# Unread products of 512 columns on TensorE behind the attention stages of a fused attention and two-layer MoE kernel

## The chip, the cores and the metric

One core of a Trainium2 chip runs the whole program. The metric is the device time of one execution in microseconds, the median of several runs. Engines are named as the profile names them: PE (TensorE's products), PEld (its weight loads), DVE (VectorE), ACT (ScalarE), POOL (GpSimd) and SP (the engine that issues most DMAs).

## The reference

Three parts run one after the other, and the output of each feeds the next:

```python
# attention: B=4, H=8, S=768, D=40; the state is D x D for each of 32 (batch, head) units
for t in range(S):
    y[:, :, t] = einsum('bhd,bhde->bhe', rt, state)
    Sa = einsum('bhde,bhe->bhd', state, at)
    state = state * wt - einsum('bhd,bhe->bhde', Sa, bt) + einsum('bhd,bhe->bhde', vt, kt)
# dense: x is y as 3072 x 320; w_in 320 x 2048, w_out 2048 x 320
h = x @ w_in
x = maximum(0.01 * h, h) @ w_out
# experts: each token goes to the one expert of eight with the largest logit
expert_idx = argmax(x @ w_gate); gate_w = softmax(x @ w_gate) at that expert
out[mask] = gate_w[mask] * (maximum(xe @ w1[e], 0) @ w2[e])
```

## The kernel before

The 768 time steps are cut into 24 chunks of 32. For a chunk `c` the work comes in two kinds. The **preparation** (`prep`, `prep_b`, `prep_c`) doesn't depend on the chunk before: scans of the decays on DVE, the scaled keys, and then two groups of small products on PE (L265, each group 16 matmuls for half of the units), which DVE and ACT take out of PSUM (L269, L271) and SP writes to memory. The **attention stages** carry the state from one chunk to the next. In the order of their use they are `s1` (L399), `s2` (L414; for chunks under 8 it is three products in a row, with an ACT copy and a DVE sum between them), `s3x` (L457), `s3` in two halves (L439), `s4` in two halves (L469), `s5` in two halves (L486) and `s6` in two halves (L504). Each is one bank of small matmuls with at most 104 rows and 80 columns of the array, followed by a copy on ACT or DVE that the next stage needs. A triangular inverse for every group of chunks (L301 to L366, on POOL, for the first group on DVE) gives the matrix `TT` that `s2` uses.

The **dense phase** is the first MoE layer, done in 12 groups of 256 tokens and 16 blocks of the hidden dimension: `layer1` is eight matmuls of 128x128 weights by 256 columns (L722), and `layer2` six of 320 columns (L738). Its weights come in as 64-bit words and are turned into pairs of float32 on DVE and ACT (L569 to L658); this conversion runs from the start of the program beside the attention. The second MoE layer (L1146, L1162) ends the program.

The order on every engine is written out by hand. `overlap` plays a string of words, `START`, and then one string for every later chunk: `s1.0` is stage `s1` of chunk 0, `0G` a piece of the preparation of chunk 0, `p` the next piece of the preparation of the chunks from 4 on, `+` a piece of the weight conversion, and `H` half a block of the dense phase. `done` counts the words `H` played so far, so it is 0 until the first one, which stands behind `s5a.2` in `START`. In the profiled execution the first product of `layer1` starts at 133.42 us. Instructions of one engine run in the order in which they were written.

A helper `keep_warm` stands in the code before, with two products, called by a word `F` that no string contains: it puts no instruction into the program. PSUM has the pool `psX` with the tags `psX0` and `psX1`, one bank each, which `layer2` sums into; nothing uses it before the first `layer2`.

Of the kernel before, what the change touches and what calls it, by code (L numbers as in the profile page):

```python
# [12 lines left out]
F32 = mybir.dt.float32  # L13
# [1233 lines left out]
def build(tc, i, out, dbg=None):  # L1247
    nc = tc.nc
    with ExitStack() as top:
# [10 lines left out]
        with ExitStack() as left, ExitStack() as ctx, ExitStack() as right:  # L1260
            psH = ctx.enter_context(tc.tile_pool(name="psH", bufs=2, space=PSUM, side="right"))
            m1 = Moe1(tc, ctx, i, k, xT, x2d, tbl, psH)
            with ExitStack() as ctx2:
                psA = ctx2.enter_context(tc.tile_pool(name="psA", bufs=4, space=PSUM))
                at = Attn(tc, ctx2, i, k, xT, bad, psA)
                own, m1.bank = m1.bank, at.bank
                half, routing = overlap(tc, at, m1, plan)
                m1.bank = own
            m2 = Moe2(tc, left, right, i, k, x2d, tbl, out, plan)

            bs = cst.tile([128, 1], F32, name="bs")
            nc.vector.tensor_reduce(out=bs, in_=bad, axis=AX.X, op=ALU.add)

            def check():
                ps = m1.bank()
                nc.tensor.matmul(ps[0:1, 0:1], bs, k.one, start=True, stop=True)
                nc.vector.tensor_single_scalar(badi[0:1], ps[0:1, 0:1], 0.0, op=ALU.is_gt)
                nc.vector.tensor_single_scalar(plan.bad, ps[0:1, 0:1], 0.0, op=ALU.is_gt)

            tail(m2, half, check)  # L1280
            m1.inner.close()
            m2.banks(m1.bank)
            m2.more()
            m2.go(routing, plan.make(m1))
# [8 lines left out]
                m2.other(lo, hi)  # L1293


def keep_warm(at, m1):

    ps = at.bank()
    for _ in range(2):
        at.nc.tensor.matmul(ps.rearrange("q (a b) -> q a b", a=4), m1.ones, m1.ones[:, None, :].to_broadcast([128, 4, 128]), start=True, stop=True)  # L1300


def overlap(tc, at, m1, plan):

    nc = tc.nc
    ws = m1.weights(at.bad[:, NC:])
    units = m1.units()
    routing, inv, hurry = [], [], []
    done = owed = 0

    def more(n):
        for _ in range(n):
            next(ws, None)


    at.scratch(m1.lend())
    for c in range(2):
        at.load1(c)
        at.load1b(c)
    at.load1b(2)  # L1320
    P = {}

    def prep():

        for c in range(4, NC):
            for n, f in enumerate(at.prep(c)):
                if n == 14 and c % 4 == 0:
                    while c // 4 - 1 not in at.read:
                        (inv if c > 4 else hurry).pop(0)()
                f()  # L1330
                if n == 3 and c + 1 < NC:
                    at.load1(c + 1)
                if n == 14:
                    if c < NC - 1:
                        at.load1b(c + 1)
                yield
            if c % 4 == 3:
                inv.extend(at.halves(1, 0, 32, nc.gpsimd) if c == 7 else at.inverse(c // 4, nc.gpsimd))

    todo = prep()  # L1340

    def half():

        nonlocal done, owed
        if done % 2 == 0:
            more(owed)
            owed = 0
            while m1.within or not m1.want(done // 2):
                next(ws, None)
            m1.flush()  # L1350
        if done == 0:
            m1.split_x()
        if done == 2 * NF:
            for _ in ws:
                pass
            m1.rows(9)
            m1.late()
        g = done // (2 * NF)
        new = next(units, None)
        if new is None:  # L1360
            return False
        done += 1
        routing.extend(new)
        if routing:
            routing.pop(0)()
            if not routing and g in EARLY:
                plan.early(m1, EARLY[g])
        if done % (2 * NF) == LOAD and g + 1 < NC // 2:
            m1.load_x(m1.xT[g + 1].rearrange("f c n -> f (c n)"))
        if done % (2 * NF) == SPLIT and g + 1 < NC // 2:  # L1370
            m1.split_x()
        return NF * NC + 3 - done

    def play(order, here=0):


        nonlocal owed
        turns, k = order.count("w"), 0
        for word in order:
            what, _, c = word.partition(".")  # L1380
            c = here + int(c or 0)
            if what[0].isdigit():
                n = int(what[0])
                if n not in P:
                    P[n] = at.prep(n)
                P[n]["abcdefGgHhIiJjz".index(what[1])]()
            elif what == "H":
                half()
            elif what == "+":
                if done % 2:  # L1390
                    owed += 1
                else:
                    more(1)
            elif what == "p":
                next(todo, None)
            elif what == "u":
                if hurry:
                    hurry.pop(0)()
            elif what == "v":
                if inv and not hurry:  # L1400
                    inv.pop(0)()
            elif what == "w":
                for _ in range(-(-len(inv) // (turns * (4 - here % 4) - k))):
                    inv.pop(0)()
                k += 1
            elif what == "L":
                at.load1(c)
            elif what == "K":
                at.load1b(c)
            elif what in "VP":  # L1410
                at.mul = nc.vector if what == "V" else nc.gpsimd
            elif what == "A":
                hurry.extend(at.halves("a", 0, 16, nc.vector))
            elif what == "B":
                hurry.extend(at.halves("b", 16, 32, nc.gpsimd))
            elif what == "C":
                m1.clear()
            elif what == "F":
                keep_warm(at, m1)
            elif what in "Ee":  # L1420
                more(what == "E")
            elif what in "gd":
                m1.low = nc.gpsimd if what == "g" else nc.vector
            elif what == "x":
                m1.load_x(m1.xT[0].rearrange("f c n -> f (c n)"))
            elif what in ("l2", "l3"):
                if c < NC:
                    (at.load2 if what == "l2" else at.load3)(c)
            elif what[2:] in ("a", "b"):
                if what[1] != "3" or c < NC - 1:  # L1430
                    getattr(at, what[:2])(c, "ab".index(what[2]))
            else:
                if what == "s2":
                    while (c // 4 if c > 3 else "ab"[c // 2]) not in at.TT:
                        (inv if c > 3 else hurry).pop(0)()
                getattr(at, what)(c)

    play(START.split())
    for c in range(5, NC):
        play((STEP if c < NC - 5 else LATE if c < NC - 1 else END).split(), c)  # L1440
    return half, routing
# [35 lines left out]
```

## Time and profile before

| What | Value |
|---|---|
| median of 3 runs | 1090.9 us (1087.32 to 1091.97) |
| the profiled execution, its own time | 1100.18 us |
| its span, first to last instruction | 1098.4 us |
| PE busy in the span | 929.3 us (85%) |
| DVE busy in the span | 807.6 us (74%) |
| mean granted clock of TensorE | 0.951 |
| first product of the dense phase | 133.42 us |

The profiled execution took 9.3 us more than the median of the runs, and 1.8 us of it lie outside its span. Busy time is the time in which an engine has at least one instruction under way. "Idle before" names what the engine waited for last. The granted clock is a column of its own in some views: 1.00 stands for TensorE's upper level of 2.4 GHz and 0.50 for its lower level of 1.2 GHz.

### The profile page before, as it was taken

The page shows a single profiled execution, that of the slowest core. Times are in us where ns is not written, and L with a number is a line of the kernel's source. Part 1 is how long each engine was busy: PE and PEld are TensorE (multiplying, and loading weights), DVE is VectorE, ACT ScalarE, POOL GpSimd, SP SyncE. Part 2 cuts the span into 40 slices and gives each one's busy share as a digit, 9 for nine tenths or more (in the row PEclk, how much of TensorE's full clock was granted, in tenths as well). Part 3 has the DMA queues.
Part 4 walks back from the last instruction along what each step waited for, and adds up shares of the span by engine and source line. Part 5 has one row for each costly group of instructions (what it writes and reads, how often), then busy time and mean ns, then how long its engine had stood idle before and what let it go on. Part 6 is the DMA issues. An engine that isn't in the chain of part 4 may idle for free.

```text
span 1098.4 us, 40672 instructions
## 1 busy us (share of the span) xinstructions
PE 929.3 (85%) x16854; PEld 871.4 (79%) x16854; DVE 807.6 (74%) x1900; ACT 531.3 (48%) x1316; POOL 512.3 (47%) x690
## 2 busy tenths in 40 slices
PE   2265778878799888889889998999999799999995
PEld 1255667777788878878779887998899699999995
DVE  8988788866778786868787666567656777877771
ACT  3545554663334444444435443444446466666661
POOL 5124145215873399447964585333556432332221
PEclk9999986888889999999999998999999899999998
DMA  7878876856546555575656442332425537354440
GB/s 250 228 213 228 227 208 178 232 149 172 151 114 173 140 162 159 141 169 138 158 151 144 124 78 73 91 82 55 151 90 140 204 129 246 100 169 146 140 126 16
DMA packets 143991, 166.04 MB, mean 151 GB/s; under 512 B 67931, under 2 KB 105451, under 8 KB 143671
## 3 DMA queue, kind: packets, MB, share of 16 engines
q1 hardware_dynamic: 133687, 144.20, 47.9%
q10 hardware_dynamic: 5760, 10.49, 3.3%
q0 software_dynamic: 4352, 8.69, 2.5%
q8 instruction: 134, 2.20, 0.9%
q14 instruction: 58, 0.48, 0.2%
HBM read 127.62 MB, written 42.27 MB: 155 GB/s over the span
## 4 chain that ended last, share of the span: by engine, by line
PE 42%; DVE 24%; DMA 9%; issue 9%; POOL 8%; ACT 6%; SPq 1%; POOLq 0%; DVEq 0%; ACTq 0%
PE psH L722 9%; PE psX L738 8%; PE epy L1162 8%; PE psH L1146 6%; DVE junk L762 3%; PE eph L1146 3%; DVE g L727 2%; POOL itmp L309 2%; POOL Tinv L315 2%; DMA L<-dKBr 2%; PE psA L414 2%; POOL gl L729 2%; DVE lam L226 1%; PE psA L486 1%; DVE Rr L472 1%
## 5 line engine op out<-in xcount | busy, mean ns | idle before, releaser
L729 POOL TENSOR_TENSOR gl<-g,gh 128x256 fp32r<-128x256 f32 x192 | 156.9, 820 | 221.4 <-ACT gh L728 186.7
L727 DVE TENSOR_TENSOR g<-psH,g 128x256 f32<-128x256 f32 x192 | 81.2, 423 | 108.2 <-ACT g L726 97.3
L728 ACT CAST gh<-g 128x256 fp32r<-128x256 f32 x192 | 78.2, 407 | 163.6 <-DVE g L727 156.7
L738 PE MATMUL psX<-woh,gh 128*128 128x320 f32 x384 | 134.0, 349 | 1.3 <-ACT woh L649 1.1
L738 PE MATMUL psX<-woh,gl 128*128 128x320 f32 x384 | 124.9, 325 | 6.9 <-POOL gl L729 6.6
L726 ACT ACTIVATE g<-psH 128x256 f32<-128x256 f32 x192 | 73.8, 384 | 109.0 <-PE psH L722 89.6
L738 PE MATMUL psX<-wol,gh 128*128 128x320 f32 x384 | 123.3, 321 | 0.0
L762 DVE SCALAR_TENSOR_TENSOR junk<-X,raws 128x320 bf16<-128x320 f32 x160 | 93.3, 583 | 4.6 <-ACT X L759 2.7
L722 PE MATMUL psH<-xh,wih 128*128 128x256 f32 x384 | 87.4, 311 | 4.9 <-DVE g L727 4.0
L309 POOL TENSOR_TENSOR itmp<-Tinv 128x30 f32<-128x30 f32 (+14 forms) x120 | 72.8, 607 | 33.9 <-DVE Tinv L301 26.7
L738 PEld LDWEIGHTS psX<-woh,gl 128*128 128x128 f32 x384 | 76.3, 199 | 10.2 <-POOL gl L729 9.7
L722 PE MATMUL psH<-xl,wih 128*128 128x256 f32 x384 | 81.3, 295 | 0.0
L722 PE MATMUL psH<-xh,wil 128*128 128x256 f32 x384 | 80.9, 294 | 0.0
L738 PEld LDWEIGHTS psX<-woh,gh 128*128 128x128 f32 x384 | 76.3, 199 | 5.4 <-ACT woh L649 1.3
L265 PE MATMUL psA<-AtI,KB 40*64 40x72 f32 x1408 | 43.9, 264 | 42.3 <-DVE KB L243 18.9
L1174 POOL DMA_INDIRECT out<-ey,sid x32 | 33.3, 1041 | 97.2 <-ACT ey L1173 91.7
L315 POOL TENSOR_TENSOR Tinv<-Tinv,itmp 128x30 f32<-128x30 f32 (+14 forms) x120 | 73.7, 614 | 7.8
L738 PEld LDWEIGHTS psX<-wol,gh 128*128 128x128 f32 x384 | 76.8, 200 | 0.3 <-DVE wol L650 0.3
L265 PEld LDWEIGHTS psA<-AtI,KB 40*64 40x64 f32 x1408 | 35.5, 163 | 49.7 <-POOL woh L242 18.3
L722 PEld LDWEIGHTS psH<-xh,wih 128*128 128x128 f32 x384 | 66.3, 201 | 10.1 <-DVE g L727 6.5
L1150 DVE SCALAR_TENSOR_TENSOR ehl<-psH,ehh 128x256 fp32r<-128x256 f32 x86 | 36.2, 421 | 41.5 <-ACT ehh L1149 38.6
L722 PEld LDWEIGHTS psH<-xl,wih 128*128 128x128 f32 x384 | 63.6, 203 | 0.3 <-DVE xl L707 0.3
(292 smaller groups left out, 2775.5 us busy)
## 6 DMA issues: line engine op xcount, KB each, us to landing
raw<-hwe SPq DMA_DIRECT2D x48, 512.0 KB
raw<-hwe SPq DMA_DIRECT2D x32, 640.0 KB
in<-h SPq DMA_DIRECT2D x23, 521.0 KB
KB<-h SPq DMA_DIRECT2D x22, 512.0 KB
L<-dKBr SPq DMA_DIRECT2D x24, 320.0 KB
dKBr<-KBr SPq DMA_DIRECT2D x22, 320.0 KB
lamY<-dl SPq DMA_DIRECT2D x24, 264.0 KB
dl<-lam SPq DMA_DIRECT2D x22, 264.0 KB
```

The costliest lines, as they stand in the source:

```text
L265: nc.tensor.matmul(box[i][64 * j:64 * j + 64, k, :], z["KB"][o, p, :], z["AtI"][o, p, :], start=True, stop=True)
L309: eng.tensor_tensor(out=box["v"], in0=T[:, k + 1:32, k:k + 1].to_broadcast([128, n, k]), in1=T[:, k:k + 1, 0:k].to_broadcast([128, n, k]), ...
L315: eng.tensor_tensor(out=T[:, k + 1:32, 0:k], in0=T[:, k + 1:32, 0:k], in1=box["v"], op=ALU.add)
L722: nc.tensor.matmul(ps[:, 0:256], w, x, start=(n == 0), stop=(n == 7))
L726: nc.scalar.activation(out=g, in_=ps[:, 0:256], func=AF.Copy, scale=0.01)
L727: nc.vector.tensor_tensor(out=g, in0=ps[:, 0:256], in1=g, op=ALU.max)
L728: nc.scalar.copy(out=gh, in_=g)
L729: return gh, gl, lambda: nc.gpsimd.tensor_tensor(out=gl, in0=g, in1=gh, op=ALU.subtract)
L738: nc.tensor.matmul(s.x2[t][:, 0:DM], x[:, o], w[:, f, :], start=(f == 0 and n == 0), stop=(f == NF - 1 and n == 2))
L762: nc.vector.scalar_tensor_tensor(out=s.junk, in0=X[:, t, 0:DM], scalar=1.0, in1=s.wg[:, e], op0=ALU.mult, op1=ALU.mult, accum_out=lg[:, t, ...
L1146: nc.tensor.matmul(ps, w, x, start=(n == 0), stop=(n == 7))
L1162: nc.tensor.matmul(s.y[t][:, 0:DM], x[:, o], w, start=(f == 0 and n == 0), stop=(f == 7 and n == 2))
```

## The change

`keep_warm` now takes the bank `psX0` and makes three products into it. The stationary operand is a 128x128 tile of ones in bfloat16, the moving operand the same tile read four times, 512 columns. Nobody reads the result. The helper is called behind both groups of products of every preparation, and behind every attention stage that `play` plays, for as long as no `H` has been played. The word `F` is gone.

```diff
-def keep_warm(at, m1):
-    ps = at.bank()
-    for _ in range(2):
-        at.nc.tensor.matmul(ps.rearrange("q (a b) -> q a b", a=4), m1.ones, m1.ones[:, None, :].to_broadcast([128, 4, 128]), start=True, stop=True)
+def keep_warm(m1):
+    ps = m1.psX.tile([128, 512], F32, name="psX0", tag="psX0")
+    for _ in range(3):
+        m1.nc.tensor.matmul(ps.rearrange("q (a b) -> q a b", a=4), m1.ones, m1.ones[:, None, :].to_broadcast([128, 4, 128]), start=True, stop=True)
...
                 f()
+                if n in (6, 10) and not done:
+                    keep_warm(m1)
...
                 P[n]["abcdefGgHhIiJjz".index(what[1])]()
+                if what[1] in "GI" and not done:
+                    keep_warm(m1)
...
-            elif what == "F":
-                keep_warm(at, m1)
...
                     getattr(at, what[:2])(c, "ab".index(what[2]))
+                    if not done:
+                        keep_warm(m1)
...
                 getattr(at, what)(c)
+                if not done:
+                    keep_warm(m1)
```

On PE this makes 45 groups of three, 135 products and 135 weight loads. The order of all other engines is the same as before, and so is PE's own beside the added instructions. On PE, from stage `s2` of chunk 0 to its first half of `s3`, there stand before:

```order
L399 MATMUL psA<-Vx_178,At 32x40 x32
L414 MATMUL psA<-RH,TT 32x40 x32
L414 MATMUL psA<-Xq,NT 32x40 x32
L414 MATMUL psA<-RH,TT 32x40 x32
L457 MATMUL psA<-ident,Xq 128x128 x4
L439 MATMUL psA<-Vx_178,L_180 40x40 x16
```

The same place as a difference, from the last product of `s2` (RH, TT) to `s3x` (ident, Xq), where `ones` is the tile of ones and `psX_825` the unread bank:

```order
 L414 MATMUL psA<-RH,TT 32x40 x32
 L414 MATMUL psA<-Xq,NT 32x40 x32
 L414 MATMUL psA<-RH,TT 32x40 x32
+L1300 LDWEIGHTS ones
+L1300 MATMUL psX_825<-ones 128x512
+L1300 LDWEIGHTS ones
+L1300 MATMUL psX_825<-ones 128x512
+L1300 LDWEIGHTS ones
+L1300 MATMUL psX_825<-ones 128x512
 L457 MATMUL psA<-ident,Xq 128x128 x4
```

Nothing stands between the three products of `s2`; the group comes behind the last. The last of the 45 groups stands on PE between the first half of `s5` of chunk 2 (L486) and the first product of the dense phase (L722):

```order
 L486 MATMUL psA<-Rr,L_180 40x32 x16
+L1300 LDWEIGHTS ones
+L1300 MATMUL psX_2214<-ones 128x512
+L1300 LDWEIGHTS ones
+L1300 MATMUL psX_2214<-ones 128x512
+L1300 LDWEIGHTS ones
+L1300 MATMUL psX_2214<-ones 128x512
 L722 MATMUL psH<-xh,wih 128x256 x2
```

From there on PE's order is that of before.

## Rows read from the trace of the kernel before

**Rows 1.** Page: busy tenths of PE and DVE in 40 slices of the span.
```profile
PE   2265778878799888889889998999999799999995
...
DVE  8988788866778786868787666567656777877771
```
**Rows 2.** Stretches: window, length, busy PE, PEld, DVE, ACT, POOL; clock, DMA share, GB/s.
```profile
18.30:53.50 35.20, 11.96 (x320) 10.08 (x320) 31.25 (x84) 16.20 (x48) 5.89 (x6) 1.00 0.80 212
61.70:133.40 71.70, 47.59 (x1484) 41.15 (x1484) 61.35 (x134) 39.43 (x108) 19.18 (x36) 1.00 0.84 227
133.40:202.20 68.80, 55.36 (x1245) 49.22 (x1246) 55.79 (x118) 37.33 (x103) 26.83 (x45) 0.75 0.75 202
```
**Rows 3.** Stretches between changes of the granted clock, same columns.
```profile
0.00:147.50 147.50, 74.97 (x2364) 64.90 (x2364) 124.83 (x277) 70.34 (x190) 44.17 (x83) 1.00 0.82 228
...
151.00:157.80 6.80, 6.08 (x79) 6.01 (x80) 6.43 (x17) 5.93 (x19) 4.49 (x11) 0.50 0.64 150
...
164.60:168.00 3.40, 3.40 (x32) 3.07 (x33) 3.40 (x5) 1.51 (x6) 2.21 (x3) 0.50 0.41 132
...
178.30:202.20 23.90, 20.22 (x435) 18.13 (x436) 18.03 (x42) 13.46 (x38) 4.95 (x8) 0.50 0.76 208
```
**Rows 4.** PE timeline 53 to 164: start, us, engine, line, out<-in [idle before <-releaser].
```profile
53.54 1.29 PE L414 MATMUL psA<-RH,TT 32*32 32x40 f32 x64 [4.19 <-DVE TT L366]
...
61.73 1.11 PE L457 MATMUL psA<-ident,Xq 128*128 128x128 f32 x4 [2.48 <-ACT Xq L427]
...
66.41 1.29 PE L439 MATMUL psA<-Vx,L 64*40 64x40 f32 x32 [0.33 <-DVE Vx L445]
67.47 1.28 PE L486 MATMUL psA<-Rr,L 64*40 64x32 f32 x32
...
77.71 1.29 PE L414 MATMUL psA<-RH,TT 32*32 32x40 f32 x64 [0.89 <-ACT RH L401]
...
81.52 1.29 PE L414 MATMUL psA<-RH,TT 32*32 32x40 f32 x64 [0.61 <-DVE RH L422]
...
163.10 0.46 PE L469 MATMUL psA<-Rr,Vt 40*32 40x32 f32 x32 [2.25 <-ACT Vt L459]
```
**Rows 5.** PE timeline: layer-2 products at the lower, then upper level; stages at the upper.
```profile
191.41 0.47 PE L738 MATMUL psX<-wol,gh 128*128 128x320 f32 x1
191.68 0.47 PE L738 MATMUL psX<-woh,gl 128*128 128x320 f32 x1
...
309.85 0.31 PE L738 MATMUL psX<-woh,gl 128*128 128x320 f32 x1
310.00 0.30 PE L738 MATMUL psX<-woh,gh 128*128 128x320 f32 x1
...
312.03 0.79 PE L439 MATMUL psA<-Vx,L 64*40 64x40 f32 x32
```
**Rows 6.** Whom PE waited for, 61.7 to 133.4: total us, times, longest.
```profile
PE psA L469 <- DMA Vt<-hvt: 4.3, 1, 4.3
PE psA L457 <- ACT Xq L427: 4.3, 2, 2.5
PE psA L399 <- issue: 2.6, 2, 1.4
...
PE psA L265 <- issue: 1.6, 1, 1.6
...
PE psA L265 <- POOL Tinv L358: 1.4, 1, 1.4
```
**Rows 7.** Whom DVE waited for, 61.7 to 133.4, same columns.
```profile
DVE Vx L426 <- PE psA L414: 2.8, 2, 1.4
```
**Rows 8.** Whom PE waited for, 133 to 235, same columns.
```profile
PE psA L414 <- ACT Xq L419: 5.7, 3, 4.6
PE psA L414 <- DVE RH L422: 4.9, 3, 2.4
...
PE psA L486 <- DMA L<-Z: 0.3, 1, 0.3
```

## The prediction

> **What bounds the kernel now.** I read the page's slices first [rows 1]: in the first five slices (some 137 us) DVE is the fuller engine, PE is half full, and from about the seventh slice on PE is at eight tenths or more. The 45 groups of unread products all lie in the first 133.4 us, so that stretch has to be weighed by itself. Between 61.7 and 133.4 us DVE is busy 61.35 of 71.7 us (86%) and PE 47.59 (66%), and from 133.4 to 202.2 us PE is busy 55.36 of 68.8 [rows 2]. DVE being full doesn't make PE free there: the longest of DVE's own waits in this stretch is for PE's `s2` [rows 7], and `s2` waits in turn for copies on ACT and DVE [rows 4]. The two hand work to each other in a fixed order, and a stage that PE makes late makes DVE late.
>
> The granted clock has to be read with care. The column says 1.00 from 0 to 147.5 us [rows 3]. The durations say otherwise: 64 products of `s2` take 1.29 us at 53.5 us and again at 77.7 [rows 4], and half an `s3` takes 1.29 us at 66.4 [rows 4] against 0.79 at 312 [rows 5], where the column shows the upper level too. So all of the stretch in question runs at the lower level, 1.2 GHz, and the first recorded change comes behind it. The Trainium skill (TensorE: Matmul & The Clock Gate, Part 1: The HAM clock gate) says that the lower level is the state an unworked TensorE starts in, and that its clock records are not fully to be trusted; the durations here agree with that and not with the column. By the column alone the change could only cost: the groups at the upper level's price, with no stage to shorten.
>
> **The change part by part.** Price of a group. No row shows a 512-column product of bfloat16. The nearest rows are `layer2`'s, 128x128 weights by 320 columns: at the lower level they start 0.27 us apart (191.41, 191.68), at the upper 0.15 (309.85, 310.00) [rows 5]. In proportion to the columns that is 0.43 and 0.24 us for 512, so a group of three costs 1.28 us at the lower level and 0.70 at the upper. The weight loads are inside those spacings, so I add nothing for them; a fresh load ahead of each group could add some 0.1 us. I take 1.28 and 0.70.
>
> What hides it. A group is free as far as PE would have waited anyway. 10 groups come before 61.7 us and 35 between there and 133.4. Of these 35 places 16 have a wait of PE behind the stage in the trace before; each can hide at most one group. The longest three are for the `Vt` transfer (4.3 us), for `Xq` (two of 4.3 together; the group behind `s2` of chunk 0 is one of the two) and for the inverse (1.4) [rows 6]. Summed place by place, with each wait capped at a group's length, 12.4 us are hidden at the lower level (1.28 each for the three long ones of 4.29, 1.79 and 1.40, and 0.2 to 1.14 for the other 13) and 9.5 at the upper. The waits inside `s2`, one of them 0.61 us in chunk 1 [rows 4], hide nothing, since no group stands there. The other 19 places have no wait: PE goes straight on, as from `s3` at 66.41 to `s5` at 67.47 [rows 4], and there the whole group pushes the next stage.
>
> At the lower level throughout: 35 x 1.28 = 44.8, less 12.4, is 32.4 us that the stretch grows by. What is left of the three long waits over a group (3.0 + 0.5 + 0.1) and two waits inside stages (1.6 and 1.4 us) [rows 6] can take up lateness from earlier, if what they wait for isn't late itself: 32.4 - 3.6 - 3.0, about 26 us at the least. I take 29.
>
> At the upper level throughout: 35 x 0.70 = 24.5, less 9.5, is 15.0 us more. The stages become shorter: 0.79 for 1.29 is 0.61 [rows 5], so 47.59 us of PE work [rows 2] would shrink by 18.6 us. If all of this counted, the stretch would end 3.6 us earlier; if half of it does, because DVE is full beside it, 5.7 us later. I take +1.
>
> The first 10 groups. In 18.3 to 53.5 us PE is busy only 11.96 of 35.2 [rows 2], and the wait of 4.19 us ahead of the first `s2` [rows 4] takes up most lateness of PE; but that wait ends with the inverse, which begins with what the first four groups of products give. Two of the early groups stand where PE goes straight on. Bounds 0 and 3 us; I take 1.5. The group behind the first `s2` is covered by the 2.48 us ahead of `s3x` [rows 4].
>
> Which level it will be. In the trace before, PE working without a break on attention stages alone never left the lower level in 133 us. It rose at 157.8, 168.0 and 202.2, each time at the end of a stretch that is full of 128x128 products, after 6.8, 3.4 and 23.9 us at the lower level [rows 3]; it fell at 164.6 [rows 3], behind a wait of PE of 2.25 us [rows 4]. A group of 1.28 us behind stages of 1.08 to 1.29 us makes half of PE's time such products where it goes straight on, so I expect rises there. But every `s2` is 5 us without a group (77.71 to 82.81) with two waits in it [rows 4], and the transfer of `Vt` leaves 3 us idle even behind a group. These three breaks (4.3 + two of about 5.5 us), each with a climb of some 5 us behind it, estimated between the 3.4 and 6.8 us of [rows 3], make 30 of 71.7 us at the lower level: 0.4.
>
> The rule of the same page (section: Why this matters for your kernels) is to leave TensorE no idle gaps between bursts, which by itself would count any busy stretch and put all of this at the upper level. The rows don't bear it out for attention stages alone, and the sum by that rule is the second rival's.
>
> After the first `H` nothing is added. PE's waits from 133 to 235 us are for ACT and DVE in the order written out, the `Xq` copies (5.7 us) and the sums of `s2` (4.9) [rows 8], both of which are late by as much; for a DMA there is 0.3 us [rows 8]. So lateness at 133.4 us is carried to the end nearly whole, and I take it as whole. That the dense phase begins at the upper level can give 0 to 2 us back, taken as 0, since PE's clock goes its own way there from `s2` to `s2`.
>
> Sum: 1.5 + 0.4 x 29 + 0.6 x 1 = 13.7 us. The profiled execution would go from 1100.18 to some 1114 us; the median of the runs is 9.3 us lower, and the same 13.7 us on it give **1104 us**, +1.2%.
>
> **The rivals.** First, the groups don't raise the clock, so the change doesn't do what it says: 1.5 + 26 to 32 us, 1118 to 1125, near 1121. For it: PE without a break stayed at the lower level all through the stretch. Against it: half of the time would be 128x128 products. Second, the upper level holds in nearly all of the stretch, and DVE paces it: 1.5 - 3.6 to 1.5 + 5.7, 1089 to 1098; as far as it lies within 5.5 us of the median it is no change. Third, the other side, faster: the upper level holds and PE's stages pace the stretch, above all `s2`, whose three products have no group between them and each lose 0.5 us. Then the 18.6 us of shorter stages count whole, the groups' 15.0 are against them, `s2` of chunk 0 (three of 1.29 us before 61.7) gives 1.5 more, and the dense phase's first 14 us, in which PE works nearly without a break, run at the upper level, which gives up to 5: down to -10 us, 1081 to 1085. It decides from about the point where less than an eighth of the stretch is at the lower level (0.125 x 29 against 0.875 x -3.6, no net loss).
>
> **How the numbers follow.** The forecast (clock goes up and down, 1097 to 1114) 0.47; the first rival 0.18; the second 0.18; the third 0.17. Half a per cent, 5.5 us, is about what a measurement of this kernel can tell from no change. Faster by more than that: the third, 0.17. Within it: most of the second and a little of the forecast's lower end, 0.20. Slower: 0.63. The range leaves out the lower half of the third rival and the upper third of the first: 1084 to 1122. The likeliest case alone is 1097 to 1114.
>
> **What the profile after would show.** The first `layer1` product at about 147 us in place of 133.4 (after allowance for the run; 160 by the first rival, 130 by the third). Unread products that start 0.43 us apart in some stretches and 0.24 in others. `s2`'s three products at 1.29 us each in most chunks, since they are what falls. DVE's waits for PE between 61.7 us and the first `H` up by about 10 us. From there to the end the same length as before, within 3 us. The forecast would be wrong if a group costs far from 1.28 and 0.70 us; if the clock stays up through `s2`; or if the dense phase takes back the lateness, which would show as a shorter stretch from the first `H` to the end.

## The result: 7.5 us slower

| | kernel before | changed kernel |
|---|---|---|
| median | 1089.54 us (1084.68 to 1095.65, 15 runs) | 1097.02 us (1091.11 to 1106.12, 15 runs) |
| profiled execution | 1100.18 us | 1098.11 us |
| its span | 1098.4 us | 1096.2 us |
| mean granted clock | 0.951 | 0.924 |
| first product of the dense phase | 133.42 us | 143.22 us |

The ratio is 1.007, with a 95% interval of 1.0045 to 1.0096: slower by more than a measurement's spread, and by about half of the forecast 13.7 us (1104 us). The two profiled executions can't be compared by their spans: that of before was 10 us over its median. So both kernels were profiled a second time, and places are compared in pairs. The two mean clocks can't be compared either: in that of before the first 147.5 us count as 1.00 [rows 3], although the durations are those of the lower level.

The page of the changed kernel, busy tenths in 40 slices, against [rows 1]:

```profile
PE   3478868878888998898989999999999899999995
...
DVE  8977678767769697877788677667657767777771
PEclk9776877688889999998999999999999899999998
```

PE is fuller in the first five slices, and DVE is emptier from the third on. The clock row now has digits under 9 from the second slice on, where the page of before had 9 in all of the first five: the first recorded change is now a rise near 28 us, and from there on the column follows the durations. The longer windows that answer to [rows 2] (window, length, busy PE, PEld, DVE, ACT, POOL with counts; clock, DMA share, GB/s):

```profile
18.30:53.50 35.20, 19.65 (x347) 10.36 (x347) 29.33 (x83) 16.17 (x48) 6.18 (x6) 0.79 0.75 201
...
61.70:133.40 71.70, 60.52 (x1396) 34.84 (x1400) 52.07 (x114) 34.23 (x93) 19.27 (x36) 0.76 0.77 205
```

PE goes from 47.59 to 60.52 us in the second window and DVE from 61.35 to 52.07. The timeline of PE in the changed kernel (start, us, engine, line, out<-in, [idle before <-releaser]) has the groups at both levels, the first rise (the preparation's products take 1.24 us at 20.89 and 0.73 at 28.65), `s2` of chunk 1, and the first dense product:

```profile
19.50 1.46 PE L1300 MATMUL psX<-ones 128*128 128x512 bf16 x3
20.89 1.24 PE L265 MATMUL psA<-woh 40*64 40x72 f32 x32
...
28.65 0.73 PE L265 MATMUL psA<-wol 40*64 40x72 f32 x32
...
67.34 0.82 PE L1300 MATMUL psX<-ones 128*128 128x512 bf16 x3
68.09 0.76 PE L469 MATMUL psA<-Rr,Vt 40*32 40x32 f32 x64
...
80.54 0.90 PE L414 MATMUL psA<-RH,TT 32*32 32x40 f32 x64 [0.58 <-ACT RH L401]
82.45 1.01 PE L414 MATMUL psA<-Xq,NT 32*32 32x40 f32 x64 [1.01 <-ACT Xq L419]
84.04 1.54 PE L414 MATMUL psA<-RH,TT 32*32 32x40 f32 x64 [0.58 <-DVE RH L422]
85.52 1.46 PE L1300 MATMUL psX<-ones 128*128 128x512 bf16 x3
...
143.22 0.50 PE L722 MATMUL psH<-xh,wih 128*128 128x256 f32 x2 [0.82 <-ACT xh L706]
```

A group takes 1.39 us of PE's time at the lower level (19.50 to 20.89) and 0.75 at the upper (67.34 to 68.09). The upper level, reached in the run of stages from 64 us on, is lost over `s2` of chunk 1: its third product and the group behind it are at lower-level lengths again.

**Where the time came from.** The stretch from 61.7 us to the dense phase falls into two parts, cut at the start of `s3x` (L457) of chunks 0 and 1 and at the first `layer1` product. The kernel before, from its two profiles, the first profile ahead:

```profile
61.73:91.04 29.31, 21.64 (x693) 18.98 (x693) 25.16 (x56) 15.96 (x45) 10.54 (x24) 1.00 0.78 207
91.04:133.42 42.38, 25.96 (x792) 22.17 (x792) 36.18 (x79) 23.47 (x64) 8.64 (x13) 1.00 0.88 241
```
```profile
61.20:89.87 28.67, 21.65 (x693) 18.98 (x693) 24.95 (x56) 15.87 (x45) 10.81 (x25) 1.00 0.76 203
89.87:133.70 43.83, 25.99 (x793) 22.36 (x793) 35.58 (x80) 23.27 (x64) 8.95 (x12) 1.00 0.85 232
```

The changed kernel, the same parts, from its two profiles:

```profile
62.44:98.04 35.60, 31.95 (x741) 18.40 (x741) 25.98 (x59) 17.50 (x49) 11.76 (x28) 0.76 0.76 204
98.04:143.22 45.18, 36.16 (x851) 20.77 (x849) 33.36 (x77) 22.11 (x59) 7.51 (x8) 0.81 0.77 206
```
```profile
62.32:97.97 35.65, 31.68 (x740) 18.16 (x741) 25.94 (x59) 17.49 (x49) 11.65 (x28) 0.76 0.70 194
97.97:139.15 41.18, 35.95 (x850) 20.55 (x849) 34.01 (x77) 22.24 (x59) 7.57 (x8) 0.79 0.81 226
```

And the groups alone (L1300) in the first of these two profiles, PE busy in the third column:

```profile
62.44:98.04 35.60, 16.77 (x48) 3.99 (x48) 0.76 0.76 204
98.04:143.22 45.18, 19.51 (x58) 4.64 (x57) 0.81 0.77 206
```

The first part grew from 29.0 us (mean of two) to 35.6: +6.6 us. There 16 groups put in 16.8 us, and the stages gave 6.5 back (21.65 less 31.95 - 16.77 = 15.2). The net of 10.3 us met a PE that had stood idle for only 7.3 us (29.0 - 21.65) and still stands idle for 3.65 and 3.97. So about half of the idle time was used, and the rest of the 10.3 us lengthens the part. The second part has 19 groups, and its mean length is the same as before, 43.2 against 43.1 us: 19.5 us of groups less 9.4 us of shorter stages is a net of 10.1, and PE had stood idle there for 16.4 and 17.8 us, of which 9.0 and 5.2 are left. The two lengths after, 45.18 and 41.18, lie 4 us apart, so the zero is known to within some 2 us only. The starts of `s3x` vary less: by the means of two profiles each, the changed kernel is 7.5 us late at `s3x` of chunk 1 (98.0 against 90.5; 0.9 of it from before chunk 0's) and 7.1 at chunk 2 (129.5 against 122.4). So nearly the whole loss is one cycle of one chunk.

DVE's waits for PE in the first part, the kernel before and then the changed one (who waits <- for whom: total us, times, longest):

```profile
DVE Ms L269 <- PE psA L265: 1.0, 1, 1.0
```
```profile
DVE Ms L269 <- PE psA L265: 4.3, 3, 1.6
DVE Rr L472 <- PE psA L469: 1.9, 1, 1.9
```

Before, its wait for the preparation's products was one of 1.0 us and for `s4` none: DVE now waits for PE. The lateness is then carried. `s3x` of chunk 10 in the first profiles of before and after:

```profile
393.13 0.66 PE L457 MATMUL psA<-ident,Xq 128*128 128x128 f32 x4
```
```profile
400.03 0.66 PE L457 MATMUL psA<-ident,Xq 128*128 128x128 f32 x4
```

In the second ones it starts at 392.32 and 399.63: +7.1 us by the means, of the same size as the 7.5 us at the end.

### The profile page after: what moved, and what is told of

Its sections match the earlier page's. It is cut to its first block, busy times and chain, and to the rows that moved or that the text cites. A ratio compares the mean times of both kernels' runs of the same rounds, so it can differ in the third digit from the quotient of the medians.

```text
span 1096.2 us, 40926 instructions
## 1 busy us (share of the span) xinstructions
PE 955.7 (87%) x16989; PEld 867.2 (79%) x16989; DVE 805.6 (73%) x1900; ACT 530.3 (48%) x1316; POOL 512.4 (47%) x690
## 4 chain that ended last, share of the span: by engine, by line
PE 47%; DVE 19%; DMA 10%; POOL 9%; issue 8%; ACT 5%; SPq 1%; ACTq 0%; POOLq 0%; DVEq 0%
PE psH L722 9%; PE psX L738 9%; PE epy L1162 8%; PE psH L1146 6%; POOL itmp L309 3%; PE eph L1146 3%; POOL Tinv L315 3%; DVE junk L762 2%; PE psA L414 2%; POOL gl L729 2%; DVE g L727 2%; PE psA L265 2%; PE psX L1300 2%; PE psA L486 1%; PE psA L439 1%
## 5 line engine op out<-in xcount | busy, mean ns | idle before, releaser
L722 PE MATMUL psH<-xh,wih 128*128 128x256 f32 x384 | 87.0, 310 | 4.8 <-DVE g L727 3.8
L722 PE MATMUL psH<-xl,wih 128*128 128x256 f32 x384 | 80.9, 294 | 0.4 <-DVE xl L707 0.4
L722 PE MATMUL psH<-xh,wil 128*128 128x256 f32 x384 | 80.6, 293 | 0.0
L722 PEld LDWEIGHTS psH<-xh,wih 128*128 128x128 f32 x384 | 66.2, 200 | 10.1 <-DVE g L727 6.1
L265 PE MATMUL psA<-AtI,KB 40*64 40x72 f32 x1408 | 39.0, 252 | 33.9 <-DVE KB L243 18.8
L265 PEld LDWEIGHTS psA<-AtI,KB 40*64 40x64 f32 x1408 | 31.3, 152 | 46.3 <-POOL woh L242 18.3
L722 PEld LDWEIGHTS psH<-xl,wih 128*128 128x128 f32 x384 | 63.4, 203 | 0.6 <-DVE xl L707 0.6
```

The source lines that it names most:

```text
L265: nc.tensor.matmul(box[i][64 * j:64 * j + 64, k, :], z["KB"][o, p, :], z["AtI"][o, p, :], start=True, stop=True)
L722: nc.tensor.matmul(ps[:, 0:256], w, x, start=(n == 0), stop=(n == 7))
```

## The experiments

Each row gives the start of the first dense product, the start of `s3x` of chunk 10, and the ratio of the times to the kernel before, with its interval. The starts come from one profile to a run, the changed kernel's from two. Before: 133.4 and 133.7 us; 393.1 and 392.3 us.

| kernel | first dense product, us | `s3x` of chunk 10, us | ratio |
|---|---|---|---|
| changed, two profiles | 143.2, 139.2 | 400.0, 399.6 | 1.007 [1.0045, 1.0096] |
| small_tile | 156.7 | 418.1 | 1.0194 [1.0138, 1.0251] |
| one_product | 136.7 | 394.6 | 0.9997 [0.997, 1.0023] |
| straight_only | 134.7 | 394.7 | 0.9979 [0.9955, 1.0004] |
| waits_only | 133.4 | 394.4 | 1.0011 [0.9978, 1.0044] |
| straight_six | 140.6 | 402.5 | 1.0084 [1.005, 1.0118] |
| after_s2_fill | 136.4 | 394.0 | 1.0043 [1.0003, 1.0083] |
| straight_s2 | 138.1 | 390.3 | 1.0 [0.9964, 1.0035] |
| s2_fill | 134.3 | 390.8 | 0.9946 [0.9908, 0.9985] |
| s2_fill_again | 132.6 | 388.0 | 0.9947 [0.9911, 0.9983] |
| s2_fill_late | 133.9 | 387.0 | 0.9949 [0.9913, 0.9986] |

**Both kernels again.** No edit. For the kernel before:

> The kernel before, once more, for a second profile. Theory (the change costs its time ahead of the dense phase and the lateness is carried): the first product of the dense phase again at 133.4 us within 1 us, and what follows it (965 us in the first profile, whose time lay 10 us over the median) nearer to 955. Rival (the groups also change what follows the first H): what follows is 965 again, against 953 in the profile after.

For the changed one:

> The changed kernel, once more. Theory: the first product of the dense phase within 2 us of 143.2, and the part behind it as long as in the kernel before, within 3 us of that run's second profile. Rival: the part behind it is shorter than before's by 10 us or so, as the first two profiles have it.

The first dense product of before came at 133.7 us, and what follows it took 958.3 us in place of 965.0. The changed kernel's came at 139.2, twice as far from its first profile as expected, and 963.3 us followed, against 953.0 in its first profile. What follows the first dense product so varies by 7 to 10 us from execution to execution in either kernel, and the pairs (965.0, 958.3) and (953.0, 963.3) don't differ by more. The rival, that the groups shorten the rest, rested on two single profiles and has no support left.

**The same groups on a 32x32 tile.**

```diff
-        ...matmul(ps.rearrange(...), m1.ones, m1.ones[:, None, :].to_broadcast([128, 4, 128]), ...)
+        ...matmul(ps[0:32].rearrange(...), m1.ones[0:32, 0:32], m1.ones[0:32, None, :].to_broadcast([32, 4, 128]), ...)
```

> The same 45 groups of three products of 512 columns, each now on a 32x32 tile of the array in place of 128x128: as long, but little of the array works. Theory (the groups raise the clock, and the shorter stages pay back most of their time): the clock stays at the lower level up to the dense phase, every stage keeps its 1.29 us, each group costs 1.28 to 1.4 us, and the kernel is 24 to 33 us slower than before, so some 17 to 25 us slower than the changed one. Rival (the clock pays nothing back, DVE paces the stretch and the groups only fill PE's free time with some overflow): the same as the changed kernel, +7 us, within 3.

The two parts of this kernel, and then two rows of its PE timeline:

```profile
62.04:105.31 43.27, 42.09 (x740) 22.57 (x740) 26.51 (x60) 17.66 (x49) 11.65 (x28) 1.00 0.60 164
105.31:156.73 51.42, 49.87 (x850) 26.45 (x849) 33.31 (x76) 22.35 (x59) 5.88 (x8) 1.00 0.77 209
```
```profile
70.64 1.46 PE L1300 MATMUL psX<-ones 32*32 32x512 bf16 x3
72.03 1.29 PE L439 MATMUL psA<-Vx,L 64*40 64x40 f32 x32
```

A group takes the same 1.39 us (70.64 to 72.03), and `s3` keeps 1.29 us: the lower level, although PE works 42.09 of 43.27 us and the column says 1.00, as ahead of any recorded change. The first dense product is 23 us late, and the end, 1.0194, some 21 us (15 to 27 by its interval), short of the 24 to 33 us named. It is far from the changed kernel's time, so the rival falls. The groups themselves cost some 23 us at the lower level, and the clock that the 128x128 groups raise pays back 13 to 18 of them. The Trainium skill (TensorE: Matmul & The Clock Gate, section Why this matters for your kernels) asks for a TensorE that is kept busy without gaps; here a TensorE on small tiles, busy for 91.96 of 94.69 us, stayed at the lower level, so that rule alone doesn't hold in this kernel.

**One product to a group.**

```diff
-    for _ in range(3):
+    for _ in range(1):
```

> One product in every group in place of three. Theory: a group of 0.43 to 0.5 us beside stages of 1.1 to 1.3 us raises the clock seldom; of 35 x 0.45 = 15.8 us the waits hide some 7, so the kernel is 5 to 9 us slower than before, about as slow as with three. Rival (the cost goes with the number of products): a third of the change's, +2.5 us. Another rival (a little work is enough to keep the clock up): faster than before by 3 to 8 us.

The first dense product is 3 us late, and the time is that of before within a quarter of a per cent. The first theory's 5 to 9 us didn't come, and the third's 3 to 8 us of gain didn't either. Ahead of the dense phase the column shows no recorded change in this run, and `s3` keeps its 1.29 us: the clock didn't rise. A third of the products cost nothing that can be measured at the end, where the change's cost divided by three would be 2.5 us: the interval reaches to +2.5, so that rival is left open. The first part is the more telling:

```profile
62.02:92.47 30.45, 28.70 (x709) 19.97 (x710) 25.38 (x57) 16.28 (x46) 12.21 (x28) 1.00 0.77 203
```

PE's work there is 28.70 us in place of 21.65, as much as the whole part was long before, and the part is 1.5 us longer.

**Half of the groups.** The groups were split by what PE did behind the stage in the trace of before: 21 where it went straight on, 24 where it waited. The number of the call decides:

```diff
 def keep_warm(m1):
+    m1.calls = getattr(m1, "calls", -1) + 1
+    if m1.calls in (1, 2, 3, 5, 6, 7, 8, 9, 13, 19, 22, 24, 25, 26, 27, 29, 30, 31, 32, 33, 35, 36, 41, 44):
+        return
```

> Of the 45 groups of three only the 21 that stand where PE, in the trace before, goes straight on to its next stage. Theory (a group costs where no wait hides it): about the whole cost of the change is here. At the measured 1.39 us per group at the lower level and 0.75 at the upper, with some 19 groups from 61.7 us on: +8 to +20 us at the first product of the dense phase, +6 to +18 at the end, as slow as the changed kernel or slower, since fewer groups raise the clock less. Rival (DVE paces the stretch, the place doesn't matter): half of the change's cost, +3 to +4.

For the other half the condition reads `not in`:

> The other 24 groups alone: those behind which PE waited anyway. Theory: hidden but for what is longer than the wait, -2 to +5 us against before at the first product of the dense phase, and a clock that seldom rises. Rival (the place doesn't matter): half of the change's cost, +3 to +4, the same as the run with the other half within 2 us.

The two parts of the stretch, in straight_only:

```profile
61.47:92.39 30.92, 25.73 (x726) 15.95 (x726) 24.86 (x56) 16.04 (x45) 10.90 (x25) 0.89 0.77 204
92.39:134.70 42.31, 29.90 (x816) 20.53 (x816) 36.16 (x79) 23.44 (x64) 8.64 (x12) 0.64 0.88 241
```

And in waits_only:

```profile
60.93:91.78 30.85, 27.23 (x708) 19.98 (x709) 26.57 (x60) 17.03 (x49) 12.04 (x28) 0.50 0.75 206
91.78:133.42 41.64, 33.70 (x827) 22.03 (x825) 34.48 (x76) 22.09 (x59) 7.00 (x8) 0.66 0.87 236
```

Neither half costs anything at the end, and the first dense product is 1.2 us late in the one and not at all in the other. This struck the theory by place, which the prediction had used: 8 to 20 us were expected of the 21 groups. The clock doesn't rescue it: with shorter stages taken off, PE's work in the two parts of straight_only still grew by 8.0 us (25.73 + 29.90 against 21.65 + 25.97), all at places without a wait, and 1.2 us came out, 2.0 by `s3x` of chunk 10. What its rival said, that the place doesn't matter, is nearer to it, but in straight_only its half of the cost didn't come either (the interval ends at +0.4 us; that of waits_only reaches +4.8). The two halves cost -2.3 and +1.2 us at the end and 2.0 and 1.7 at `s3x` of chunk 10, where both together cost 7.5 and 7.1: the cost isn't a sum over places. In the first part PE has 21.65 us of work before, 25.73 and 27.23 with one half, and 31.8 with both. With one half it still fits into a part of 30.9 us, with both it doesn't. (The 0.89 of straight_only counts the time ahead of its first recorded change, near 66 us, as 1.00; `s3` takes 1.29 us there.) The reading that fits is that a stage that is late behind a group is late only until PE's next wait, which is that much shorter, whether or not a group stands in that wait.

**Twice as many products at half of the places.** A second theory was formed from this, of PE's waits as one common store, and tried on the 21 straight-on places:

```diff
-    for _ in range(3):
+    for _ in range(6):
```

> The 21 groups at the places where PE goes straight on, with six products each in place of three, which is as much added PE time as the changed kernel's 45 groups of three. Theory by place, the prediction's (each product there costs its whole time): 19 groups longer by 0.75 us at the upper level, +14 us over the run with three, so +11 to +17 against before at the first product of the dense phase. Theory of a common store (PE's waits from 61.7 us to the first H, 24 us in all, take up lateness wherever the groups stand, until some 10 are left): no more than the changed kernel's, +2 to +8 us at the first product of the dense phase, and from 1 us faster to 7 slower at the end.

```profile
62.75:96.95 34.20, 31.61 (x758) 18.39 (x758) 24.07 (x54) 16.41 (x45) 12.18 (x28) 0.87 0.66 179
96.95:140.60 43.65, 32.51 (x845) 20.89 (x841) 36.08 (x82) 23.40 (x64) 6.36 (x8) 0.77 0.83 233
```

The first dense product is 7 us late, inside the 2 to 8 us of the store and outside the 11 to 17 us by place; the end, 1.0084, is some 9 us late and passes the 7 us named. The first part is the telling one: PE's work is 31.61 us, as in the changed kernel (31.95), from other groups at other places, and the part is 34.20 us long against 35.6. The store isn't one over the whole stretch, though: the second part has 11.1 us of idle time left, which the first part can't draw on. That it is one to each chunk's cycle is argued from these two parts.

Ordered by PE's work, the first parts of all these kernels read:

| kernel | PE's work, us | length of the first part, us | idle, us |
|---|---|---|---|
| before, two profiles | 21.64, 21.65 | 29.31, 28.67 | 7.67, 7.02 |
| straight_only | 25.73 | 30.92 | 5.19 |
| waits_only | 27.23 | 30.85 | 3.62 |
| one_product | 28.70 | 30.45 | 1.75 |
| straight_s2 (below) | 28.95 | 32.86 | 3.91 |
| straight_six | 31.61 | 34.20 | 2.59 |
| after_s2_fill (below) | 31.81 | 35.96 | 4.15 |
| changed, two profiles | 31.95, 31.68 | 35.60, 35.65 | 3.65, 3.97 |
| small_tile | 42.09 | 43.27 | 1.18 |

Up to about 29 us of work the part grows by at most 2 us, with one exception (straight_s2), and with more work it grows, from whatever places this comes. It isn't a sharp limit: some 1 to 5 us stay idle, and they differ from kernel to kernel, so the balance tells which part will pay and not, to a microsecond, how much. In the second part PE's work of up to 36.2 us goes with lengths of 39 to 45 us in no order.

**Two more products in each wait inside `s2`**, written into the bank that the next product of `s2` overwrites. In the changed kernel for chunks 0 to 2:

```diff
         def times(M, at, x, fill=0):
             ps = s.bank()
+            for _ in range(fill):
+                nc.tensor.matmul(ps.rearrange("q (a b) -> q a b", a=4), s.ones, s.ones[:, None, :].to_broadcast([128, 4, 128]), start=True, stop=True)
...
-            ps = times(s.NT, 8 * (c % 4), lambda sl, g: Xv[sl, g // 4, g % 4, :])
+            ps = times(s.NT, 8 * (c % 4), lambda sl, g: Xv[sl, g // 4, g % 4, :], 2 if c < 3 else 0)
...
-        ps = times(TT, 8 * (c % 4), lambda sl, g: s.RH[sl, g, :])
+        ps = times(TT, 8 * (c % 4), lambda sl, g: s.RH[sl, g, :], 2 if c < 3 else 0)
...
+    at.ones = m1.ones
```

> The changed kernel with two more products in each of the two waits inside s2, for chunks 0 to 2, the only ones ahead of the dense phase. Theory (s2 without a group is the place where the clock falls): the lower level's share from 61.7 us to the first H sinks from 0.48 to under 0.3, each s2 loses up to 1.5 us, and the first product of the dense phase comes 3 to 8 us earlier than in the changed kernel, at 133 to 139 us; at the end 0 to 4 us slower than before. Rival (DVE and the place of the groups set it, the clock doesn't): the same as the changed kernel, +7 us.

```profile
61.13:97.09 35.96, 31.81 (x745) 17.57 (x746) 26.55 (x60) 17.47 (x49) 11.90 (x28) 0.81 0.73 197
97.09:136.40 39.31, 32.33 (x854) 18.47 (x852) 32.44 (x75) 22.05 (x59) 8.71 (x8) 0.96 0.86 235
```

In the second part the clock stays up (0.96), and the part is 39.31 us, 4 us shorter than the mean of either kernel (43.1, 43.2) and 1.9 us shorter than the shortest of their four profiles. In the first part nothing is won: a clock of 0.81 for 0.76, and PE as full as in the changed kernel. At the end 1.0043 lies between before and the changed kernel, and its interval lets both theories stand. By the starts the theory is borne out: the first dense product comes at 136.4 us against 143.2 and 139.2, and `s3x` of chunk 10 at 394.0 against 400.0 and 399.6.

Without the groups, the same products inside `s2` for chunks 0 to 7 (`2 if c < 8 else 0`), twice:

> No groups. In place of them two products of 512 columns in each of the two waits inside s2, for chunks 0 to 7, so also behind the first H: into the bank that the next product of s2 then overwrites. Theory (s2 is what falls to the lower level, and its waits hide 0.9 us): the first product of the dense phase within 2 us of before, the lower level between 178 and 202 us shorter, the kernel 2 to 6 us faster. Rival (the clock behind s2 is set by what stands around it, and PE's waits there are short): no difference, or 1 to 4 us slower.

> The kernel with two products in each wait inside s2 (chunks 0 to 7) and no groups, again, with more rounds. If its lead over before is real: ratio 0.993 to 0.998. If it was the runs' spread: 0.998 to 1.002.

And for chunks 3 to 7 alone, all behind the first dense product (`2 if 3 <= c < 8 else 0`):

> The same products inside s2 only for chunks 3 to 7, so only behind the first H, where PE's clock alternates. Theory (the lead comes from PE's clock behind the first H, where PE's stages and the dense products are what the rest waits for): the whole of the other run's lead, ratio 0.993 to 0.998. Rival (it comes from the three s2 ahead of the dense phase): ratio 0.998 to 1.003.

All three are faster than the kernel before, by 0.5%, as their theories had it. The last has no added product ahead of the first `H` and shows as large a lead, so nothing that can be told apart comes from ahead of it. Two windows behind the first `H`, of the second profile of before and then of s2_fill_late:

```profile
178.30:202.20 23.90, 20.08 (x444) 17.57 (x435) 18.39 (x41) 13.13 (x38) 6.09 (x11) 0.51 0.75 207
235.00:310.00 75.00, 59.15 (x1463) 54.48 (x1453) 51.60 (x124) 29.25 (x80) 44.61 (x63) 0.89 0.57 155
```
```profile
178.30:202.20 23.90, 20.78 (x464) 17.53 (x468) 18.64 (x43) 13.98 (x39) 5.70 (x9) 0.65 0.74 209
235.00:310.00 75.00, 63.84 (x1519) 57.30 (x1518) 54.11 (x131) 31.40 (x85) 49.90 (x70) 0.93 0.56 156
```

In both windows the clock is higher, and between 235 and 310 us PE, DVE, ACT and POOL get more done: DVE 54.11 us of work for 51.60. `s3x` of chunk 5 starts at 234.52 and 235.67 us in the two profiles of before and at 234.15 here, that of chunk 7 at 309.06 and 310.05 against 303.97; s2_fill and s2_fill_again have 306.49 and 305.09 there. So the lead arises mostly between chunks 5 and 7. Products that nobody reads can only add work, so the higher clock is the likely cause; which stage gains isn't traced further. These versions are faster than both kernels.

**The straight-on groups and the products inside `s2` together:**

> The 21 groups of three where PE goes straight on together with the products inside s2 for chunks 0 to 7. Theory (both keep the clock up at places the other leaves out, and PE's waits still take up the groups): first product of the dense phase at 131 to 135 us, ratio 0.990 to 0.997, the fastest of all. Rival (the waits inside s2 are then used up, and the groups' lateness comes out): first product at 136 to 140 us, ratio 0.998 to 1.004.

```profile
60.83:93.69 32.86, 28.95 (x730) 17.21 (x730) 25.06 (x56) 15.90 (x45) 11.97 (x28) 0.95 0.65 176
```

Its rival held at the first dense product (138.1 us) and at the end (1.0), and the theory's fastest kernel of all didn't come. The part behind the first dense product, 951.4 us in this one profile, lies within the 7 to 10 us by which that length varies, and `s3x` of chunk 10 is early, at 390.3 us. That the groups ahead take what the products inside `s2` give behind is likely by the end, and not shown. What makes the first part 32.86 us long with 28.95 us of work for PE stays open.

## Why the prediction came out as it did

**The reading of the clock** was right. The stretch ran at the lower level, and the column's 1.00 ahead of a first recorded change is no measurement: small_tile shows 1.00 beside an `s3` of 1.29 us, the length of [rows 4]. One reading was too strong: PE didn't work "without a break" in that stretch of before, it stood idle for 24.1 of 71.7 us [rows 2]. What was concluded from it, that the attention stages alone don't raise the clock, holds in small_tile even for a PE busy 91.96 of 94.69 us.

**The price of a group** was 1.28 and 0.70 us, worked out from `layer2` [rows 5]; it is 1.39 and 0.75. The 0.1 us that was named for a first weight load and left out is there at the lower level; what makes it up isn't shown.

**The first 10 groups** were put at 1.5 us. `s3x` of chunk 0 starts at 62.44 and 62.32 us after 61.73 and 61.20: +0.9.

**The share of the lower level** was put at 0.4. The clock of the two parts, 0.76 and 0.80, is a share of 0.48 and 0.40. That it rises in runs of stages and falls over `s2` was right: the three falls recorded between 62 us and the dense phase, near 83, 104 and 124 us, are at the three breaks named, `s2` of chunks 1 and 2 and the wait for `Vt`.

**The term at the lower level** was put at 29 us, with 26 as its least. small_tile, which is that rival made into a kernel, is 23.2 us late at the first dense product, 0.6 of it from before 62 us: 22.6. So it was mis-sized, by 6.4 us, which at a share of 0.4 is 2.6 us of the sum. It had taken each wait as the cover of the one group that stands in it, and the waits that went on paying for other groups' lateness as 3.6 + 3.0 us. In small_tile PE's idle time in the stretch sinks from 24.1 us [rows 2] to 2.7: nearly all of it is given, whatever stands where.

**The term at the upper level**, +1 us, has no run of its own. The nearest part is the second one of after_s2_fill, with a clock of 0.96: 4 us shorter than before. The prediction's lower bound for the whole stretch was -3.6. An estimate by the prediction's own sum: of the 6.7 us (mean of two profiles) that the stretch grew by, 0.44 x 22.6 = 9.9 belong to the lower level, which leaves -3.2, or -5.7 for a whole stretch at the upper level (some -2 and -9 by the single profiles of the changed kernel). So this term was too high as well, by the means by more than the other, and probably for the same reason: the 9.5 us hidden were counted place by place.

**The sum** was 13.7 us at the first dense product; 9.8 and 5.5 were measured, the mean 7.6. The time of 1097.0 us lies at the lower edge of the span named as likeliest (1097 to 1114); the way was right, the size nearly twice too large. By parts the first one came out: with the prediction's own prices and places, its 16 groups come to 17.3 us at the lower level (20.5 less 3.2 hidden) and 0.4 at the upper, 7.2 us at a share of 0.4, and 6.6 were measured. That agreement is luck as far as places go, since the same counting fails for the 11 groups of straight_only in that part (PE's work grew by 4.1 us, the part by 1.9) and for one_product. The second part carries most of the miss: some 5 us are left for it in the prediction's sum, 0 measured, since there PE had 17 us of idle time for 19 groups. **The step that failed** is thus the one under "What hides it": each wait was taken to hide at most the group that stands in it, while the runs show PE's waits within a cycle taking up lateness from other places, up to about 29 us of work in the first part. The prediction also summed both parts in one line and so didn't see that in one of them PE was already three quarters full (21.65 of 29.0) and in the other at 0.6 (26 of 43).

**The carry** to the end, taken as whole, was right: +7.1 us at chunk 10, +7.5 at the end.

**What the profile after was to show.** The first `layer1` product was put at 147 us and came at 143.2 and 139.2. By the lengths of groups of three and of single products, the products of a group start some 0.43 and 0.22 us apart, where 0.43 and 0.24 were named. `s2` falls within its three products and not ahead of them: 0.90, 1.01 and 1.54 us in chunk 1, 0.79, 1.29 and 1.29 in chunk 2, where 1.29 was named for each. A rest of unchanged length within 3 us can't be told from single profiles: the means are 961.7 us before and 958.2 after, in lengths that vary by 7 to 10. DVE's waits for PE between 61.7 us and the dense phase went from 6.9 us in all to 15.5, up by 8.6 where about 10 were named.

**The rivals.** The first, a clock that stays low, needs small products and is then 21 us slower at the end, where 27 to 34 were given. The second, an upper level in nearly all of the stretch, would need a clock nearer to 1 than 0.76 and 0.80. The third, faster, was priced from -10 us on; where the clock does stay up, as in the second part of after_s2_fill, one part gives some 4 us, and the first part, 7 us longer than before, takes them.

## What to carry to other kernels

Filler work on a waiting engine isn't charged by the place at which it stands but by the balance of each dependent cycle: take the engine's work in one cycle, add the filler, take off what a higher clock gives back, and compare with the cycle's length. As long as idle time is left over, little is paid; what would fill the cycle is paid for the most part, and here this began some us before it was full. So put filler where a cycle has idle time to spare, cut the stretch into cycles before summing, and try the waits of the stage at which the clock falls: here two products in each of the two waits inside `s2`, for five chunks beside the dense phase, gave 0.5%, where 135 products behind every stage ahead of it cost 0.7%.

## What the runs showed of the hardware

In small_tile PE is busy 91.96 of 94.69 us, with stages on tiles of up to 104x40, groups on 32x32 and only the four products of each `s3x` on 128x128, and doesn't leave the lower level, while the same groups on 128x128 raise it, first near 28 us, in the run of groups and preparation products that starts at 18.33. The granted clock's column reads 1.00 ahead of the first recorded change also where the stages have lower-level lengths (133 us of them in before, 156 in small_tile); the length of a known stage tells the level. And the level changes the length of the small attention stages by a factor of 0.61 (1.29 to 0.79 us), not by half, while a group goes from 1.39 to 0.75.
